# Two attention products in 64x32 tiles of the TensorE array, with units of every second head

## The chip, the cores and the metric

The kernel runs on one core of a Trainium2 chip. The metric is device microseconds from the start to the end of one execution. A core has five engines, each working through its own instructions in order: TensorE (PE, matmuls; its weight loads are shown as PEld), VectorE (DVE), ScalarE (ACT), GpSimd (POOL) and SyncE (SP, which issues the DMAs here). PE reads SBUF and writes PSUM, which has eight banks of 2 KB on each of 128 partitions. TensorE's clock is granted at one of two levels, 2.4 or 1.2 GHz; the profile writes them as 1.0 and 0.5.

## The reference

```python
batch, n_heads, seq, head_dim = (8, 8, 576, 64); n_mem = 32
def _attn_ref(q, k, v, phi):
    a = exp(phi - phi.max(axis=2)); a = a / (a.sum(axis=2) + 1e-09)     # over the 576 positions
    k_m, v_m = einsum('bhsm,bhsd->bhmd', a, k), einsum('bhsm,bhsd->bhmd', a, v)
    attn = softmax(q @ k_m.T / sqrt(64))                                 # over the 32 slots
    return attn @ v_m
def _moe_ref(x, w_in, w_out):  h = x @ w_in; return (h - tanh(h)) @ w_out     # 512 -> 2048 -> 512
def _moe2_ref(x, w_in, w_out): h = x @ w_in; return where(h > 0, h, exp(min(h, 0)) - 1) @ w_out
x = attn_out.transpose(0, 2, 1, 3).reshape(4608, 512); x = _moe_ref(x); x = _moe2_ref(x)
```

The weights come as 64-bit floats. Everything is computed to about fp32 accuracy.

## The kernel before

The program has an attention part, a first layer and a second layer. The attention runs beside the first half of the first layer, the second layer follows.

**Attention** works in 16 units: one batch `b` and four heads each (`Attention.unit`). A unit takes the maximum and the exponential of `phi`, forms `km` (k_m and v_m of its four heads, 32 array columns for each head), transposes q (`pq`) and k_m, v_m (`kT_ps`), forms the scores `sc`, and writes the probabilities `p`, each value as a high and a low part, to DRAM. The scores of two heads at a time are one product over all 128 rows of the array: `kT` holds the slots of a head twice, beside zeros, so that one pass serves two halves of q. A unit has two such products side by side (64 columns each) for each pair of heads, each into one bank.

**First layer.** v_m and w_in are multiplied first: `vw` = v_m times w_in, so that h = p times `vw`. w_in is cut in 8 column groups `pg` of 256, the work in 4 sweeps `sw` of two groups and 16 blocks `n` of 288 tokens, two blocks for each batch. The loop over `blocks` (index `bi`, 64 of them) does two steps `i` in each, one for each `pg`. A step is `h_unit` (12 matmuls, `h_ps`), the function h - tanh(h) on ACT, POOL and DVE (`g_a` to `g_d`), and up to two `x_unit`s of earlier blocks (12 matmuls each, `x_ps`, `x_next`). For the groups 0 to 3 `vw_whole` forms `vw` for one batch from plain fp32 operands, in two column halves of the array, with a v_m that holds zeros beside each head's block (`vbd`). For the groups 4 to 7 `vw_half` does it for two batches at once from high and low parts of v_m and w_in, three matmuls for each product. v_m is saved to DRAM and loaded again for the second half (`save_vm`, `load_vm`, `split_vm`).

**Conversion.** `convert` makes fp32 from the 64-bit weights, 128x512 words in a piece: one ACT and four DVE instructions through the one PSUM buffer of `cv_ps`; with `whole` the result stays fp32, otherwise ACT and POOL split it in high and low. Pieces are started by `Staged.round`, one in two rounds, from the queue `first` before the queue `todo`. `need(kind, pg)` runs rounds on the spot until the two pieces of a group are there. `raw_p` holds three pieces.

**What sets the order.** Each engine takes its instructions as the program issues them: `units.at` holds the round in which each unit begins, every `yield` of a unit ends one round, and `cv.round` advances the conversions. `misc`, three PSUM banks, serves `x_ps`, `vw_ps` and the attention's tiles alike; the product of `h_unit` has four banks of its own. `keep_busy` issues matmuls without a use, in places listed in `beside`.

Of the kernel before, what the change touches and what calls it, by code (L numbers as in the profile page):

```python
# [8 lines left out]
F32 = mybir.dt.float32  # L9
# [63 lines left out]
class Attention:  # L73
# [5 lines left out]
    def __init__(self, tc, ctx, const, ins, vm_dst, p_dram, side, psum):  # L79
        nc = tc.nc  # L80
        self.nc, self.ins, self.vm_dst, self.p_dram = nc, ins, vm_dst, p_dram
        self.ident, self.pmask, self.ones = const["ident"], const["pmask"], const["ones"]
# [16 lines left out]
        nc.gpsimd.memset(self.kT, 0.0)  # L99

    def load(self, u, what):
# [4 lines left out]
        view = lambda n, h0, n_h: self.ins[n][b, 4 * g + h0:4 * g + h0 + n_h].rearrange("h (p c) d -> p h c d", c=6)  # L106
# [12 lines left out]
    def unit(self, u, nxt, eng, first_p=None):  # L119
# [15 lines left out]
        beside = {("km", 2): 10, ("bmax", 3): 10, ("km", 3): 5, ("sc1", 2): 5, ("sc0", 3): 9, ("bmax", 5): 3}  # L135
# [42 lines left out]
        twice = lambda t: kmv[:, t].rearrange("p (o d) -> p o d", o=1).to_broadcast([128, 2, D])  # L178
# [9 lines left out]
        s = self.sc_p.tile([128, 18, M], F32, tag="s", name="s")  # L188
        for pr in range(2):
            qt = self.loaded.pop((u, f"q{pr}"))  # L190
            qT = wk.tile([128, 2, 3, 96], F32, tag="qT", name="qT")
            for h in range(2):
# [4 lines left out]
                nc.scalar.activation(qT[:, h], pq, ACTF.Copy)  # L197
# [3 lines left out]
            if pr == 0:  # L201
                kT_ps = ps_tile([128, 2, 128], "kT_ps")
                nc.tensor.transpose(kT_ps[:, 0, :], kk.rearrange("p h d -> p (h d)"), ident)
                nc.tensor.transpose(kT_ps[:, 1, :], vbd.rearrange("p h d -> p (h d)"), ident)
                for cp in range(2):
                    r = slice(64 * cp, 64 * cp + 64)
                    nc.scalar.activation(kT[r, :, cp, :], kT_ps[r, 0, :].rearrange("p (h m) -> p h m", h=4), ACTF.Copy)
                dst = self.vm_dst(b, g)
                src = kT_ps[:, 1, :].rearrange("p (r m) -> p r m", r=2)
                nc.scalar.activation(dst, src, ACTF.Copy)  # L210
                self.vm_done.add(u)
                yield
            sc_t = ps_tile([128, 512], "sc")
            sc = sc_t[:, :NB]
            for hq in range(2):
                if hq == pr:
                    keep_busy(nc, ident, sc_t[:, 384:], beside.get((f"sc{pr}", u), 0))
# [16 lines left out]
        pTv = r32(phl[:, :, 1])  # L234
        for r in range(2):
            nc.vector.transpose(pTv[:, r], s[:, 9 * r:9 * r + 9].rearrange("p j m -> p (j m)"))
        yield
        nc.scalar.activation(phl[:, :, 0], pTv, ACTF.Copy)
        eng.tensor_tensor(phl[:, :, 1], pTv, r32(phl[:, :, 0]), op=ALU.subtract)
# [3 lines left out]
        for c, t in enumerate(first_p or ()):  # L243
# [8 lines left out]
def make_const(nc, const):  # L252
# [3 lines left out]
    for h in range(4):  # L256
        for j in range(2):
            nc.vector.memset(pmask[32 * h:32 * h + 32, j:j + 1], 1.0 if h % 2 == j else 0.0)
# [696 lines left out]
```

## Time and profile before

| | |
|---|---|
| median of 3 runs | 1677.83 us (1676.79 to 1677.95) |
| span of the profiled execution | 1680.0 us |
| PE busy | 1616.5 us, 96% of the span |
| DVE, ACT, POOL busy | 1197.3, 930.9, 759.7 us |
| matmul records | 10038 |

The page gives the span of the profiled execution alone; what lies around it is in no view. A fp32 matmul stands in the trace as two records, a matmul of high and low parts as one. A line of a profile group reads: line of the source, engine, operation, output and inputs by name, shapes, count, then busy time (overlaps counted once) and the mean of one in ns, then the idle time of the engine before them and what ended it. A line of a timeline reads: start, time from the first start to the last end, engine, line, what it does, count, and in brackets the idle time before it with its releaser.

### The profile page before, as it was taken

The numbers are of one execution on the slowest core, as the hardware profiler recorded it, in microseconds if no ns is written. First come the engines' busy times: TensorE is split into PE (matmuls) and PEld (weight loads), VectorE is DVE, ScalarE is ACT, GpSimd is POOL, SyncE is SP. The second block draws the span as 40 slices with busy tenths as digits, with TensorE's granted clock in tenths as the row PEclk, the third lists the DMA queues.
The fourth block names the chain that finished last, engine by engine and source line by source line (L and its number), as shares of the span: only waits on it lengthen the run. The fifth ranks groups of instructions, "written<-read, shape, count | busy, mean of one in ns | idle before, by whom it ended". The sixth has DMA issues, their size and how long they took to land.

```text
span 1680.0 us, 26878 instructions
## 1 busy us (share of the span) xinstructions
PE 1616.5 (96%) x10038; PEld 1403.2 (84%) x10038; DVE 1197.3 (71%) x1746; ACT 930.9 (55%) x1677; POOL 759.7 (45%) x540
## 2 busy tenths in 40 slices
PE   6779999899999999999999999999999999999998
PEld 4558888787899999999999888888888888888886
DVE  6877688877989999999765655656565555555654
ACT  2546767777788898988853333333333333333332
POOL 1335656666767676767642322322232232323222
PEclk9889999999999999999999999999999999999999
DMA  9865667676565566665586321212121212121100
GB/s 237 211 188 169 208 194 232 194 230 208 192 199 174 171 220 217 218 220 193 174 319 253 101 76 38 88 38 75 47 67 51 63 51 64 50 76 51 32 7 25
DMA packets 140922, 236.10 MB, mean 141 GB/s; under 512 B 8184, under 2 KB 102392, under 8 KB 138744
## 3 DMA queue, kind: packets, MB, share of 16 engines
q1 hardware_dynamic: 140792, 234.39, 43.8%
q8 instruction: 79, 1.29, 0.3%
q14 instruction: 51, 0.42, 0.1%
HBM read 158.73 MB, written 74.45 MB: 139 GB/s over the span
## 4 chain that ended last, share of the span: by engine, by line
PE 70%; DVE 4%; issue 2%; ACT 2%; POOL 1%; DMA 0%; DVEq 0%; SPq 0%; POOLq 0%; ACTq 0%
PE h_ps L486 24%; PE o_ps L528 24%; PE x_ps L426 14%; PE h_ps L375 7%; PE vw_ps L344 1%; DVE s L403 1%; DVE vw L349 1%; DVE h_ps L402 1%; PE vw_ps L360 0%; DVE x L434 0%; DMA raw<-in_moe_w_in_dram 0%; DVE xr L460 0%; ACT t L386 0%; ACT vw L347 0%; ACT u L387 0%
## 5 line engine op out<-in xcount | busy, mean ns | idle before, releaser
L512 POOL TENSOR_TENSOR e<-hm,e 128x512 fp32r<-128x512 f32 x144 | 187.1, 1299 | 577.7 <-ACT e L511 534.5
L426 PE MATMUL x_ps<-g,w 128*128 128x288 f32 x3072 | 441.2, 297 | 7.4 <-ACT x L432 3.3
L426 PEld LDWEIGHTS x_ps<-g,w 128*128 128x128 f32 x3072 | 417.6, 189 | 20.2 <-ACT x L432 5.7
L486 PE MATMUL h_ps<-x,wi 128*128 128x512 f32 (+1 forms) x1920 | 424.6, 371 | 0.0
L528 PE MATMUL o_ps<-wo,e 128*128 128x512 f32 x1728 | 422.8, 393 | 0.7 <-POOL e L512 0.7
L486 PEld LDWEIGHTS h_ps<-x,wi 128*128 128x128 f32 x1920 | 336.1, 188 | 68.0
L528 PEld LDWEIGHTS o_ps<-wo,e 128*128 128x128 f32 x1728 | 323.4, 188 | 75.3 <-POOL e L512 1.1
L497 ACT ACTIVATE t_ps<-hm 128x512 f32<-128x512 f32 x144 | 86.7, 602 | 505.8 <-DVE hm L496 505.8
L393 POOL TENSOR_TENSOR v<-t,u 128x576 f32<-128x576 f32 x128 | 183.4, 1433 | 143.4 <-ACT u L387 134.3
L503 DVE SCALAR_TENSOR_TENSOR hm<-hm,t_ps 128x512 f32<-128x512 f32 x144 | 99.1, 688 | 200.3 <-ACT hm L498 200.3
L411 POOL TENSOR_TENSOR g<-s,g 128x576 fp32r<-128x576 f32 x128 | 200.6, 1567 | 81.1 <-ACT g L410 78.6
L375 PE MATMUL h_ps<-p,vw 128*128 128x288 f32 x1536 | 230.9, 299 | 1.3 <-DMA p<-phl 1.3
L375 PEld LDWEIGHTS h_ps<-p,vw 128*128 128x128 f32 x1536 | 210.8, 189 | 11.5 <-issue 8.1
L496 DVE TENSOR_SCALAR hm<-h_ps 128x512 f32<-128x512 f32 x144 | 99.6, 692 | 130.7 <-PE h_ps L486 129.7
L403 DVE SCALAR_TENSOR_TENSOR s<-s,v 128x576 f32<-128x576 f32 x128 | 146.5, 1144 | 6.3 <-POOL v L393 6.3
L386 ACT ACTIVATE t<-h_ps 128x576 f32<-128x576 f32 x128 | 83.4, 651 | 76.1 <-PE h_ps L375 31.7
L404 DVE COPY_PREDICATED s<-big,h_ps 128x576 f32<-128x576 uint32 x128 | 106.7, 834 | 11.8
L388 ACT ACTIVATE s<-u,bias 128x576 f32<-128x576 f32 x128 | 99.6, 778 | 26.0 <-POOL g L411 17.1
L505 DVE TENSOR_TENSOR hm<-hm,h_ps 128x512 f32<-128x512 f32 x144 | 98.9, 687 | 5.0
L504 DVE SCALAR_TENSOR_TENSOR hm<-hm,t_ps 128x512 f32<-128x512 f32 x144 | 98.9, 687 | 4.9
L498 ACT ACTIVATE hm<-hm 128x512 f32<-128x512 f32 x144 | 91.0, 632 | 13.1
L397 ACT ACTIVATE big<-u,bias 128x576 f32<-128x576 f32 x128 | 98.0, 765 | 0.1
(98 smaller groups left out, 1716.4 us busy)
## 6 DMA issues: line engine op xcount, KB each, us to landing
x_dram<-x SPq DMA_DIRECT2D x128, 288.0 KB
xr<-x_dram SPq DMA_DIRECT2D x72, 512.0 KB
p<-p_dram SPq DMA_DIRECT2D x62, 576.0 KB
raw<-in_moe_w_in_dram SPq DMA_DIRECT2D x32, 512.0 KB
raw<-in_moe_w_out_dram SPq DMA_DIRECT2D x32, 512.0 KB
w_dram<-wst SPq DMA_DIRECT2D x32, 512.0 KB
kv<-in_k_dram SPq DMA_DIRECT2D x16, 576.0 KB
kv<-in_v_dram SPq DMA_DIRECT2D x16, 576.0 KB
```

Of the source, the lines that this page charges most:

```text
L375: nc.tensor.matmul(ps[:, j, :NB], lhsT=vw[a][:, kc, 128 * j:128 * j + 128], rhs=p[:, kc, b, :], start=(k == 0), stop=(k == 5))
L388: nc.scalar.activation(s, u, ACTF.Square, bias=bias[:, 0:1], scale=G_S)
L393: nc.gpsimd.tensor_tensor(v, t, u, op=ALU.mult)
L403: nc.vector.scalar_tensor_tensor(s, s, G_B, v, op0=ALU.add, op1=ALU.mult)
L404: nc.vector.copy_predicated(s, big.bitcast(U32), d)
L411: nc.gpsimd.tensor_tensor(g[:, 1], s, r32(g[:, 0]), op=ALU.subtract)
L426: nc.tensor.matmul(ps, lhsT=wo[pg][a][:, j, 128 * dm:128 * dm + 128], rhs=self.g[n, pg][:, b, j, :], start=(k == 0), stop=(k == 11))
L486: nc.tensor.matmul(out, lhsT=w3[:, a, kc, 128 * j:128 * j + 128], rhs=x[:, b, kc, :], start=(i == 0), stop=(i == 11))
L496: nc.vector.tensor_scalar(hm, w[0], 0.0, None, op0=ALU.min)
L503: nc.vector.scalar_tensor_tensor(hm, hm, 1.0, t, op0=ALU.add, op1=ALU.mult)
L512: nc.gpsimd.tensor_tensor(e[:, 1], hm, r32(e[:, 0]), op=ALU.subtract)
L528: nc.tensor.matmul(acc, lhsT=e[:, a, jj, 128 * tg:128 * tg + 128], rhs=w4[:, b, j, :], start=(k == 0 and jj == 0 and i == 0), stop=(k == l ...
```

## The change

A unit now takes every second head of a batch (`view` reads `(h j)`, the unit's `g` picks `j`). k_m and v_m come out of the transpose in both halves of the partitions (`kvs`, formed by one instruction), so that the products can run in tiles of 64 rows and 32 columns: eight tiles hold four heads times two row halves, and no zeros are needed. The scores of all four heads are formed at once, after both pairs of q are transposed, into two banks. `vw_unit` replaces `vw_whole` and `vw_half`: one batch, one sweep (two groups `pg`), eight tiles in two banks, all from fp32. All eight groups of w_in stay whole fp32, v_m stays in SBUF, and its saving, loading and splitting are gone. `vw_unit` stands at each odd `bi`, for the next pair of blocks, between the step's two `x_unit`s. For the first two units the parts of `p` are written straight into the tiles that `h_unit` reads. The groups 4, 5 and 6, 7 of w_in are queued at block 26 and 30, not 24 and 28.

```diff
-        self.kT = fix.tile([128, 4, 2, M], F32, name="kT")
+        self.kT = fix.tile([128, 4, M], F32, name="kT")
...
-        kk = wk.tile([128, 2, D], F32, tag="kk", name="kk")
-        nc.vector.tensor_scalar(kk, twice(0), rs, None, op0=ALU.mult)
-        vbd = wk.tile([128, 2, D], F32, tag="vbd", name="vbd")
-        for j in range(2):
-            nc.vector.tensor_scalar(vbd[:, j], kmv[:, 1], rs, self.pmask[:, j:j + 1], op0=ALU.mult, op1=ALU.mult)
+        kvs = wk.tile([128, 2, 2, D], F32, tag="kvs", name="kvs")
+        twice = kmv[:, :2].rearrange("p t (o d) -> p t o d", o=1).to_broadcast([128, 2, 2, D])
+        nc.vector.tensor_scalar(kvs, twice, rs, None, op0=ALU.mult)
...
-            sc_t = ps_tile([128, 512], "sc")
-            sc = sc_t[:, :NB]
-            for hq in range(2):
-                nc.tensor.matmul(sc[64 * hq:64 * hq + 64], lhsT=kT[:, 2 * pr + hq].rearrange("p c m -> p (c m)"),
-                                 rhs=qT[:, hq].rearrange("p c q -> p (c q)"), start=True, stop=True)
-            nc.vector.transpose(s[:, 9 * pr:9 * pr + 9].rearrange("p j m -> p (j m)"), sc)
-            yield
+        sc = [ps_tile([128, 512], "sc") for _ in range(2)]
+        for h in range(4):
+            for cp in range(2):
+                r = slice(64 * cp, 64 * cp + 64)
+                nc.tensor.matmul(sc[cp][32 * h:32 * h + 32, :NB], lhsT=kT[r, h, :],
+                                 rhs=qT[r, h].rearrange("p c q -> p (c q)"), start=True, stop=True)
+        for cp in range(2):
+            nc.vector.transpose(s[:, 9 * cp:9 * cp + 9].rearrange("p j m -> p (j m)"), sc[cp][:, :NB])
+        yield
...
+    def vw_unit(self, vm, wi, b, pgs):
+        hi, lo = self.vw[b % 2, pgs[0] // 2]
+        ps = [self.misc.tile([128, 512], F32, tag="m", name="vw_ps") for _ in range(2)]
+        for pg in pgs:
+            cols = slice(256 * (pg % 2), 256 * (pg % 2) + 256)
+            for h in range(4):
+                for j in range(2):
+                    r = slice(64 * j, 64 * j + 64)
+                    nc.tensor.matmul(ps[j][32 * h:32 * h + 32, cols], lhsT=vm[r, b % 2, h, :], rhs=wi[pg][r, h, :],
+                                     start=True, stop=True)
+        cols = slice(256 * (pgs[0] % 2), 256 * (pgs[-1] % 2) + 256)
+        for j in range(2):
+            nc.scalar.activation(hi[:, j, cols], ps[j][:, cols], ACTF.Copy)
+            nc.vector.tensor_tensor(lo[:, j, cols], ps[j][:, cols], r32(hi[:, j, cols]), op=ALU.subtract)
...
-            staged, whole = [], (layer, kind) == (1, "i") and pg < 4
+            staged, whole = [], (layer, kind) == (1, "i")
...
-            if bi == 24:
+            if bi == 26:
                 cv.first.extendleft(reversed(conv_l1("i", 4, 5)))
-            if bi == 28:
+            if bi == 30:
                 cv.first.extendleft(reversed(conv_l1("i", 6, 7)))
...
+                if vw_next and (bi == 1 or i == 0):
+                    vb, vsw = vw_next
+                    pgs = [2 * vsw + i] if bi == 1 else [2 * vsw, 2 * vsw + 1]
+                    for vpg in pgs:
+                        need("i", vpg, bi == 1)
...
+                    make_vw(vb, pgs)
```

Three places show how it moves instructions.

On SP, the DMAs around the first two units' stores: `in_moe_w_out` rows are the pieces of w_out, two for each group, `in_moe_w_in` those of w_in. Before:

```order
L603 DMA raw<-in_moe_w_out_dram 128x512
L246 DMA p<-phl 32x1152 x4
L247 DMA p_dram<-phl 128x1152
L246 DMA p<-phl 32x1152 x4
L247 DMA p_dram<-phl 128x1152
L116 DMA q<-in_q_dram 96x2x384
L603 DMA raw<-in_moe_w_out_dram 128x512
L113 DMA phi<-in_phi_dram 96x4x192
L600 DMA raw<-in_moe_w_in_dram 128x2x256
```

The two rows of w_out are the third and the fourth of it, with which the groups 0 and 1 are complete, ahead of w_in's groups 2 and 3. After:

```order
L575 DMA raw<-in_moe_w_out_dram 128x512
L242 DMA p_dram<-p 128x576 x2
L572 DMA raw<-in_moe_w_in_dram 128x2x256
L116 DMA q<-in_q_dram 96x2x384
L113 DMA phi<-in_phi_dram 96x4x192
L321 DMA p<-p_dram 128x1152
```

The third piece of w_out stands where it stood, but w_in's group 2 comes next. A unit has one `yield` less, so the opening has one round less, and the fourth piece (group 1) stays in `todo`, behind all that block 0 puts in `first`.

On DVE, around the `vw` of group 2 in block 1 (L50 to L57 are one conversion, the L57 row ends it). Before:

```order
L54 SCALAR_TENSOR_TENSOR cv_m<-raw,cv_m 128x512
L57 SCALAR_TENSOR_TENSOR w_838<-raw,cv_m 128x512
L236 STREAM_TRANSPOSE phl<-s 128x288 x2
L145 TENSOR_REDUCE nmax<-mT 128x1
L363 TENSOR_TENSOR vw<-vw_ps,vw 128x512
L402 TENSOR_TENSOR h_ps<-h_ps,t 128x2x288
```

After:

```order
L342 TENSOR_TENSOR vw<-vw_ps,vw 128x256 x2
L50 TENSOR_SCALAR cv_m<-cv_m 128x512
L51 TENSOR_SCALAR cv_m<-cv_m 128x512
L54 SCALAR_TENSOR_TENSOR cv_m<-raw,cv_m 128x512
L57 SCALAR_TENSOR_TENSOR w_862<-raw,cv_m 128x512
```

The four conversion rows stand seven times in a row there before the next `h_ps` row: both pieces of w_in's group 3, four pieces of w_out's groups 2 and 3, and last the fourth piece of w_out, which the first `x_unit` needs. On PE that `x_unit` stands right behind this `vw`, as before.

On DVE, in block 31, the first with a `vw` of group 4 and 5. Before, ahead of the first `vw` of that sweep:

```order
L434 COPY x<-x_ps 128x288
L402 TENSOR_TENSOR h_ps<-h_ps,t 128x2x288
L403 SCALAR_TENSOR_TENSOR s<-s,v 128x576
L404 COPY_PREDICATED s<-big,h_ps 128x576
L349 TENSOR_TENSOR vw<-vw_ps,vw 64x512 x2
```

After:

```order
L384 COPY_PREDICATED s<-big,h_ps 128x576
L54 SCALAR_TENSOR_TENSOR cv_m<-raw,cv_m 128x512
L57 SCALAR_TENSOR_TENSOR w_6312<-raw,cv_m 128x512
L342 TENSOR_TENSOR vw<-vw_ps,vw 128x512 x2
L414 COPY x<-x_ps 128x288
```

The last piece of group 5 (`w_6312`) now ends right before the evictions of the product that reads it. On PE the product stands behind the first of the step's two `x_unit`s. Block 35 has the same for group 7.

## Rows read from the trace of the kernel before

**Rows 1.** Stretches: limits, length, busy of the five engines, PEclk, DMA share, GB/s.

```profile
97.61:152.66 55.05, 45.05 (x388) 37.18 (x386) 44.73 (x75) 35.34 (x71) 30.64 (x22) 0.96 0.58 176
152.66:430.00 277.34, 259.71 (x2194) 225.77 (x2191) 219.33 (x342) 206.41 (x415) 176.69 (x126) 1.00 0.68 212
430.00:512.00 82.00, 81.17 (x604) 75.33 (x603) 74.41 (x105) 65.97 (x115) 56.66 (x40) 1.00 0.59 192
512.00:830.00 318.00, 316.83 (x2386) 314.73 (x2385) 295.48 (x418) 281.34 (x488) 222.74 (x155) 1.00 0.57 199
830.00:1680.00 850.00, 843.13 (x3962) 699.78 (x3961) 494.18 (x677) 305.60 (x516) 251.72 (x177) 1.00 0.24 80
```

**Rows 2.** Groups by line: `vw` matmuls of fp32 parts, a conversion's low part, evictions of `vw`.

```profile
L64 POOL TENSOR_TENSOR w<-cv_a,w 128x512 fp32r<-128x512 f32 x24 | 31.5, 1312 | 0.0
...
L344 PE MATMUL vw_ps<-w,vms 128*128 128x256 f32 x192 | 28.7, 285 | 1.2 <-DVE vw L349 1.0
...
L363 DVE TENSOR_TENSOR vw<-vw_ps,vw 128x512 fp32r<-128x512 f32 x32 | 21.7, 682 | 30.1 <-ACT vw L362 30.1
...
L362 ACT ACTIVATE vw<-vw_ps 128x512 fp32r<-128x512 f32 x32 | 18.8, 592 | 14.5 <-PE vw_ps L360 14.5
```

**Rows 3.** Timeline of PE, 303 to 323 us.

```profile
303.37 0.71 PE L218 MATMUL sc<-qT,kT 128*64 128x288 f32 x4
304.01 1.86 PE L426 MATMUL x_ps<-g,w 128*128 128x288 f32 x12
...
313.70 1.75 PE L426 MATMUL x_ps<-g,w 128*128 128x288 f32 x12
315.38 1.08 PE L360 MATMUL vw_ps<-w,vm 128*64 128x256 f32 x8
316.40 1.86 PE L426 MATMUL x_ps<-g,w 128*128 128x288 f32 x12
319.32 2.16 PE L170 MATMUL km<-kv,a 96*32 96x192 f32 x48 [1.06 <-ACT a L163]
321.41 1.08 PE L360 MATMUL vw_ps<-w,vm 128*64 128x256 f32 x8
```

**Rows 4.** Timeline of PE, 601 to 624 us.

```profile
601.73 0.88 PE L344 MATMUL vw_ps<-w,vms 128*128 128x256 f32 x6
602.44 1.78 PE L375 MATMUL h_ps<-p,vw 128*128 128x288 f32 x12
...
620.43 3.36 PE L426 MATMUL x_ps<-g,w 128*128 128x288 f32 x24
623.63 1.77 PE L375 MATMUL h_ps<-p,vw 128*128 128x288 f32 x12
```

**Rows 5.** Timeline of DVE, the same stretch.

```profile
619.57 0.69 DVE L57 SCALAR_TENSOR_TENSOR cv_a<-raw,cv_m 128x512 uint32<-128x512 uint32 x1
...
622.06 0.83 DVE L404 COPY_PREDICATED s<-big,h_ps 128x576 f32<-128x576 uint32 x1
```

**Rows 6.** Timeline of PE: the first `h_unit`, the first `x_unit`, the ninth block step.

```profile
59.95 1.86 PE L375 MATMUL h_ps<-p,vw 128*128 128x288 f32 x12 [1.35 <-DMA p<-phl]
...
94.56 3.25 PE L426 MATMUL x_ps<-g,w 128*128 128x288 f32 x12
97.61 0.68 PE L195 MATMUL pq<-ident,q 96*128 96x96 f32 x3
...
152.66 1.85 PE L375 MATMUL h_ps<-p,vw 128*128 128x288 f32 x12
```

**Rows 7.** Timeline of ACT: the first instruction of three conversions.

```profile
28.34 0.64 ACT L48 ACTIVATE cv_m<-raw 128x512 f32<-128x512 f32 x1 [0.92 <-DVE w L57]
...
31.93 0.63 ACT L48 ACTIVATE cv_m<-raw 128x512 f32<-128x512 f32 x1 [1.87 <-DVE w L57]
...
38.40 0.63 ACT L48 ACTIVATE cv_m<-raw 128x512 f32<-128x512 f32 x1 [5.36 <-DMA raw<-in_moe_w_in_dram]
```

**Rows 8.** Timeline of DVE: the end of w_in's group 2.

```profile
87.98 0.69 DVE L57 SCALAR_TENSOR_TENSOR w<-raw,cv_m 128x512 uint32<-128x512 uint32 x1
```

More of the change, by code (lines that the diff above doesn't have):

```diff
@@ L254, in make_const @@
     make_identity(nc, ident)
-    pmask = const.tile([128, 2], F32, name="pmask")
-    for h in range(4):
-        for j in range(2):
-            nc.vector.memset(pmask[32 * h:32 * h + 32, j:j + 1], 1.0 if h % 2 == j else 0.0)
     ones = const.tile([128, 96], F32, name="ones")
@@ L329, in load_p, with new_vw @@
         self.nc.sync.dma_start(out=r32(t).rearrange("p r t s -> p (r t s)"),
-                               in_=self.p_dram[n // 2, :, :, n % 2].rearrange("g q m f -> (g q) m f"))
-    def vw_half(self, vm, wi, pg, po):
+                               in_=self.p_dram[n // 2, n % 2].rearrange("p g f -> p (g f)"))
+    def new_vw(self, b, sw, slot):
+        self.vw[b % 2, sw] = [self.vw_p.tile([128, 2, 512], F32R, tag=f"vw{slot}{t}", name="vw") for t in range(2)]
+    def vw_unit(self, vm, wi, b, pgs):
@@ L333, in vw_half @@
         nc = self.nc
-        pars = range(2)
-        if po == 0:
-            for par in pars:
-                pool = self.vw2_p if self.vw2_p and par and pg // 2 % 2 else self.vw_p
-                self.vw[par, pg] = [pool.tile([128, 2, 256], F32R, tag=f"vw{pg % 2}_{par}{t}", name="vw")
-                                    for t in range(2)]
-        ps = self.misc.tile([128, 2, 256], F32, tag="m", name="vw_ps")
-        for kc in range(2):
-            p = 2 * po + kc
-            for i, (a, b) in enumerate(((0, 0), (0, 1), (1, 0))):
-                nc.tensor.matmul(ps[:, kc], lhsT=vm[:, a, p, :], rhs=wi[b][:, p, :], start=(i == 0), stop=(i == 2))
@@ L370, in h_unit @@
             keep_busy(nc, self.const["ident"], ps[:, 1, 384:], 9)
+        c0 = 256 * (pg % 2)
         for j in range(2):
@@ L563, in moe_kernel @@
         new = lambda stack, name, n, **kw: stack.enter_context(tc.tile_pool(name=name, bufs=n, reuse_waits="tile", **kw))
-        l1a, l1b, l1c, at0_ctx, at1_ctx, wt_ctx, late_ctx, pro, ps_h_ctx = (ExitStack() for _ in range(9))
+        l1a, l1b, l1c, at0_ctx, at1_ctx, wt_ctx, pro, ps_h_ctx = (ExitStack() for _ in range(8))
         m1 = Moe1(tc, l1a, const, p_dram, x2_dram)
         wt_p = {0: new(l1b, "wt0", 1, side="right"), "early": new(l1a, "wte", 1)}
-        vm_p = new(l1b, "vm", 2, side="right")
-        vms_p = new(l1b, "vms", 1, side="right")
+        vm_p = new(l1b, "vm", 1, side="right")
         cv_p = new(l1b, "cv", 2, side="right")
@@ L613, in dst @@
                         if kind == "i":
-                            ws[pg] = [wt_p[pg2 % 2].tile([128, 4, 256], F32 if whole else F32R, tag=f"wi{odd}a", name="w1")]
-                            if not whole:
-                                ws[pg].append(wt_p[2].tile([128, 4, 256], F32R, tag=f"wl{pg}", name="w1"))
+                            ws[pg] = [wt_p[pg2 % 2].tile([128, 4, 256], F32, tag=f"wi{odd}a", name="w1")]
                         else:
@@ L693, in moe_kernel @@
         blocks += [(ss, bp, sub, j) for ss, bp, sub in groups[4:] for j in range(4)]
-        vw_first = {4 * b + 2 * sub - 1: (b, sub) for b in range(4) for sub in range(2)}
         LAG = 4
@@ L806, in moe_kernel @@
                 nxt = (2 * nss + nsub, 4 * nbp + nj)
[L808 to L816 removed]
+            vw_next = None
+            if bi % 2 and nxt:
+                vw_next = (nxt[1] // 2, nxt[0])
             if at0_open:
@@ L866, in moe_kernel @@
                     m1.g_d(*pend.pop())
[L867 to L870 removed]
+                if vw_next and (bi == 1 or i == 0):
[3 more added lines that the diff above has]
+                        need("i", vpg, bi == 1)
                     while not all(u in vm_done for u in range(2 * vb + 2)):
                         units.round()
[L873 to L879 removed]
+                    if i == 0:
+                        m1.new_vw(vb, vsw, bi // 2 % 2 ^ 1)
+                    make_vw(vb, pgs)
                 if soon and bi > 60:
```

149 lines of the change are left out of this document (37 added, 112 removed).

## The prediction

> **What bounds the kernel now.** I read the stretches first [rows 1], to see which engine is full where. PE is busy 259.71 of 277.34 us from 152.66 to 430, 81.17 of 82 up to 512, 316.83 of 318 up to 830 and 843.13 of 850 in the second layer, which the change does not touch. So from 152.66 on, PE time that goes is time that goes, unless a new wait takes its place. DVE is next: 295.48 of 318 in the saturated stretch. Ahead of 152.66 it is different: from 97.61 on PE is busy for 45.05 of 55.05 us, the rest are waits for conversions and for the attention. There PE work is worth little and the order of the other engines much. Then I read the timelines of PE for the price of one product [rows 3, 4], those of the opening [rows 6 to 8] for what the new order does, and DVE's timeline and groups [rows 2, 5] for the evictions. The result is worked out as a difference and taken off the median, 1677.8; the profiled span, 1680.0, is 0.1% longer.
>
> **The price of a product in array tiles.** A `vw` of the old kind has 8 records in two column halves, four behind one another in each, 256 columns wide, and the next instruction starts 316.40 - 315.38 = 1.02 us after it [rows 3]. A scores product has two records behind one another, 288 columns wide, and takes 304.01 - 303.37 = 0.64 us. From 1024 k + o = 1.02 and 576 k + o = 0.64 come k = 0.85 ns for a column of one record and o = 0.15 us. `km` tests this: 48 records in four column tiles, 12 in each of 192 columns, give 2304 x 0.85 + 150 = 2.11 us, and 321.41 - 319.32 = 2.09 was measured. So column tiles work side by side at no cost, and it is the records of one tile that count. Around such a product PE loses some more: 0.08 us ahead of it (the `x_unit` before it holds PE 315.38 - 313.70 = 1.68 us; two of them undisturbed take 3.20, so 1.60) and 0.11 us behind it (1.86 for the next `x_unit`, against 1.75) [rows 3, 4]. A `vw` product costs 1.21 us in all, a scores product 0.83.
>
> **What goes on PE**, if the two row halves work side by side as the column tiles do. Before, groups 0 to 3 have 32 products of 1.21 = 38.7 us. After, 14 pairs of groups have four records in each tile, 1.21 each; the two single groups of the opening stand side by side, 1.21; the two of block 1 stand apart, 512 x 0.85 + 150 = 0.59 and 0.19 for the edges, 1.56. Sum 19.7, less by 19.0. Groups 4 to 7 have 32 products of 602.44 - 601.73 = 0.71 us [rows 4], 22.7 in all, with no edges since they use the whole array; after, 16 pairs of 1.21 are 19.4, less by 3.3. Scores: 32 of 0.83 before, 16 after, less by 13.3. Together 35.6 us of PE. Row halves side by side are in no row of this trace. Below, the cost may be what it would be one after the other, which is the second rival; I take the value next to the column tiles. The Trainium skill ("TensorE: Matmul & The Clock Gate", Part 3, Packing small matmuls) says that tiles in different rows and columns run concurrently; no run here shows it for rows, and by that page the sum is the one I use.
>
> **Up to the ninth step (152.66 before).** Behind this mark lie 26 of the old `vw` of groups 0 to 3, 13 pairs now, and 21 of the old scores products, 11 now: 13 x 1.21 + 10 x 0.83 = 24.0 us less. The other 19.0 + 13.3 - 24.0 = 8.3 lie ahead of it, and I expect them to be swallowed. The order rows show why: the fourth piece of w_out now waits in `todo`, and the first `x_unit` calls for it in block 1, so six other pieces are converted first, seven in a row, with PE standing. One conversion takes 31.93 - 28.34 = 3.59 us from first instruction to first instruction, with the one PSUM buffer [rows 7]. Before, w_in's group 2 was done at 87.98 + 0.69 = 88.7 [rows 8]. The opening gets some 2.5 us shorter: the first `h_unit` waited 1.35 us for the DMA of `p` [rows 6], which now needs none, and one conversion's half less stands ahead (bounds 0 and 4). From 86.2, seven conversions reach 111.3; the high part on ACT, about as long as the 0.64 of a conversion's first instruction, and the low part on POOL, 1.31 [rows 2], put it at 113.3. The `x_unit` ended at 97.6 before [rows 6]. From there to the ninth step PE had 45.05 us of work in 55.05; now 1.6 less for `vw`, 1.7 less for scores, 1.0 less since it ran partly at the lower clock level (0.96 in the row), 1.9 more for matmuls of `keep_busy` that stood earlier before: 42.6 us. Six of the conversions that DVE had here are done, so I fill PE as in the next stretch, 259.71 / 277.34 = 0.94: 45.5 us. The ninth step comes at 159, 6 us later. Bounds: with the idle share of before (55.05 less 45.05 = 10 us) it comes 13 us later; with PE full and the opening 4 us shorter, at the old time. Also one unit's `km` (2.1 us) has moved behind this mark.
>
> **From there to 830.** PE gets 24.0 + 3.3 - 2.1 = 25.2 us shorter. What is late instead:
> First, banks. `misc` has three. A `vw` or scores product now holds two. In the two steps in which `km` still holds the third, the `x_unit` right behind `vw` gets a bank that this `vw` has just filled, and waits for ACT's copy and DVE's subtraction, 592 and 682 ns [rows 2], and for what DVE has ahead of it: 2.2 us each, 4.4. Some five times the next small product takes a bank whose scores DVE has yet to transpose, 0.6 each, 3. Together 7.5 (bounds 2, if DVE is free each time, and 14, if its queue is as long as in the saturated stretch).
> Second, blocks 31 and 35. The last piece of group 5, then of group 7, ends on DVE right ahead of its use. In the nearest step of before, the copy on DVE that stands ahead of it ends at 622.89 and two conversion instructions of 0.70 follow, 624.3 [rows 5]; PE would be at the product after the first `x_unit`, 620.43 + 1.60 = 622.0 [rows 4]. Wait 2.3 each, 4.6 (bounds 2 and 7).
> Third, in the rest of the saturated stretch PE waited 1.0 us for DVE's `vw` [rows 2]; that goes, since 64 evictions of 64 rows become 32 of 128. The second `x_unit` of a step now needs the bank of the first, whose copy ends about when `vw` does: 0.2 each time, 16 times. Net 1.5 (bounds -1 and 6).
> ACT and POOL lose eight splits and the four of v_m, and SP the seven DMAs of v_m; they are not on the path and count nothing.
>
> **Sum.** 6 - 25.2 + 7.5 + 4.6 + 1.5 = -5.6 us, so 1677.8 - 5.6 = 1672.
>
> **Rivals.**
> (a) Everything is gained: seven conversions cost nothing net, because PE idled there anyway, and DVE is early at each bank. 0 - 25.2 + 2 + 2 - 1 = -22: 1656, and down to 1642 if the 8.3 and the opening come back too. For it: PE is 99% full where most of the gain lies. Chance 0.14.
> (b) The other side: the row halves take turns. Then every tile pair has twice the records: 30 x 1024 x 0.85 ns = 26 for the pairs, 2 for the singles, 16 x 576 x 0.85 = 8 for the scores, 36 us more: 1708. It turns slower once the halves overlap by less than about five sixths. For it: no row shows row tiles. Against it: records of different column tiles start next to each other at no cost. Chance 0.11.
> (c) The burst is longer. A conversion waited 5.36 us for its piece [rows 7]; if DMA makes each of the seven 4.5 us, not 3.6, that is 6 us more, and PE, idle so long, comes back at the lower level, 2 to 4 more: 1681. Chance 0.15.
> (d) The evictions become the bound: every pair waits for its copies, 592 + 682 ns, 30 times 1.27 = 38, of which 4.4 and 3.2 are in the sum: 1702. For it: DVE is at 93% in the saturated stretch. Against it: it loses 32 x 0.68 us there, and only at two places does the next tile need that bank. The Trainium skill ("TensorEngine Tiling (Array Packing)", PSUM Bottleneck) warns of exactly this: array tiles speed up TensorE and not the emptying of PSUM. The trace has one sign for it, the 1.0 us on DVE's `vw` above. Chance 0.05.
>
> **How the numbers follow.** The forecast has 0.55. Its own bounds, 13, 14, 7 and 6 at one end and 0, 2, 2 and -1 at the other, do not meet all at once; 1660 to 1686 holds most of it. The range goes to (a) and past (c) and leaves out (b), (d) and the end of (a): 1651 to 1692. A difference of 0.2%, 3.4 us, is about what a measurement can tell. Of the forecast I count 0.40 as faster, 0.08 same and 0.07 slower, of (c) 0.03, 0.05 and 0.07, (a) is faster, (b) and (d) slower: faster 0.57, same 0.13, slower 0.30.
>
> **What would show it.** `vw` at 1.02 us for 16 records of each pair on PE (twice that in case b); scores at 0.64 once for each unit; a gap of 20 us or more on PE ahead of the first `x_unit`, released by a conversion's low part, and seven conversions 3.6 us apart under it; the ninth `h_unit` near 159; 2 us waits for DVE in blocks 31 and 35; the second layer unchanged. A ninth step at 152 or earlier, or PE idle of over 25 us between it and 430, would prove the sum wrong.

## The result and the profile after

The changed kernel takes 1696.1 us (1695.1 to 1697.9), the kernel before 1677.9 in the same series: ratio 1.0104, 95% interval 1.009 to 1.0118. It is slower by 18 us, where 1672 was forecast, and the time lies above the range. Steps are counted by the starts of the first layer's `h_unit`s, from 0; the ninth is step 8, step 127 is the last. The stretches of both traces between the same steps (limits, length, busy of PE, PEld, DVE, ACT and POOL, PEclk, DMA share, GB/s), after first:

```profile
60.00:160.11 100.11, 63.10 (x608) 53.17 (x607) 69.94 (x109) 49.65 (x97) 40.70 (x29) 0.80 0.50 147
160.11:521.58 361.47, 331.19 (x3122) 296.08 (x3121) 277.97 (x428) 267.75 (x522) 230.38 (x164) 0.98 0.66 207
521.58:600.79 79.21, 77.51 (x670) 73.64 (x669) 69.13 (x97) 61.83 (x109) 46.56 (x33) 1.00 0.51 173
600.79:622.82 22.03, 17.61 (x110) 17.16 (x109) 14.83 (x22) 12.66 (x23) 9.75 (x8) 0.85 0.33 103
622.82:874.58 251.76, 249.25 (x2151) 240.24 (x2150) 202.80 (x296) 200.37 (x355) 174.44 (x118) 1.00 0.61 207
874.58:1694.00 819.42, 812.39 (x3770) 674.29 (x3768) 472.24 (x653) 287.22 (x485) 236.07 (x167) 1.00 0.23 75
```

```profile
60.00:152.66 92.66, 73.35 (x610) 58.35 (x610) 73.08 (x122) 52.92 (x105) 44.35 (x32) 0.91 0.67 186
152.66:508.31 355.65, 337.19 (x2767) 297.41 (x2764) 290.19 (x440) 269.34 (x524) 230.07 (x163) 1.00 0.66 207
508.31:586.65 78.34, 78.11 (x590) 77.50 (x589) 73.98 (x108) 69.40 (x121) 54.48 (x39) 1.00 0.54 175
586.65:602.44 15.79, 15.79 (x122) 15.79 (x121) 15.28 (x22) 14.57 (x27) 14.07 (x10) 1.00 0.59 217
602.44:855.59 253.15, 252.21 (x1899) 250.72 (x1897) 231.65 (x320) 219.15 (x380) 173.02 (x120) 1.00 0.60 211
855.59:1680.00 824.41, 817.54 (x3770) 674.19 (x3768) 472.30 (x653) 286.87 (x485) 236.16 (x167) 1.00 0.23 74
```

Step 8 comes 7.45 us later; from there to step 60, where most was to be gained, the changed kernel needs 5.8 us more: PE is busy 6.0 us less and idle 11.8 us more (30.3 against 18.5). Steps 75 to 78 lose 6.2; the rest of the first layer gains 0.5, the part from step 127 on 5.0. That sums to the 14.1 by which the profiled spans differ (the profiled execution of before is the longest of its four, 1681.4).

**The price** is as forecast. PE's timeline in the saturated stretch (start, length, idle before it and releaser):

```profile
626.11 1.09 PE L337 MATMUL vw_ps<-w,vm 64*32 64x256 f32 x32
627.14 1.87 PE L406 MATMUL x_ps<-g,w 128*128 128x288 f32 x12
```

The next instruction starts 1.03 us after the pair, and the pair does the work of two old products of 1.02 [rows 3]. Undisturbed scores take 0.65 us for a whole unit, what one of its two products took before. In noburst, a run described below, it reads:

```profile
100.06 0.72 PE L212 MATMUL sc<-qT,kT 64*32 64x288 f32 x16
100.70 1.86 PE L355 MATMUL h_ps<-p,vw 128*128 128x288 f32 x12
```

The row halves work side by side.

**The burst** is as forecast too. PE around the first `x_unit`, and ACT's first instruction of two of the conversions:

```profile
84.14 2.53 PE L406 MATMUL x_ps<-g,w 128*128 128x288 f32 x9
110.88 0.61 PE L406 MATMUL x_ps<-g,w 128*128 128x288 f32 x1 [24.21 <-ACT w L62]
112.68 0.85 PE L406 MATMUL x_ps<-g,w 128*128 128x288 f32 x2 [1.19 <-POOL w L64]
```

```profile
84.81 0.66 ACT L48 ACTIVATE cv_m<-raw 128x512 f32<-128x512 f32 x1
88.42 0.62 ACT L48 ACTIVATE cv_m<-raw 128x512 f32<-128x512 f32 x1 [2.95 <-DVE w L57]
```

The conversions are 3.61 us apart (3.59 in [rows 7]). The instruction behind the `x_unit` starts at 113.3 (forecast 113.3; 97.6 before, [rows 6]), and step 8 at 160.1 (forecast 159).

**What was not forecast** is inside the pairs. PE and ACT around one of them:

```profile
239.70 0.38 PE L200 MATMUL kT_ps<-ident,kvs 128*128 128x128 f32 x2
240.76 0.62 PE L337 MATMUL vw_ps<-w,vm 64*32 64x256 f32 x2 [0.69 <-ACT x L412]
241.75 1.09 PE L337 MATMUL vw_ps<-w,vm 64*32 64x256 f32 x30 [0.37 <-ACT vm L203]
242.77 1.86 PE L406 MATMUL x_ps<-g,w 128*128 128x288 f32 x12
```

```profile
239.64 0.78 ACT L368 ACTIVATE s<-u,bias 128x576 f32<-128x576 f32 x1
240.32 0.39 ACT L412 ACTIVATE x<-x_ps 128x288 f32<-128x288 f32 x1
240.61 0.76 ACT L377 ACTIVATE big<-u,bias 128x576 f32<-128x576 f32 x1
241.28 0.26 ACT L201 ACTIVATE kT<-kT_ps 128x128 f32<-128x128 f32 x1
241.44 0.26 ACT L203 ACTIVATE vm<-kT_ps 64x128 f32<-64x128 f32 x1
```

The pair's first matmul waits for the bank of the `x_unit` ahead, which ACT copies (`x`, L412) behind its work for the function h - tanh(h), called the gate below. Its second writes the other bank, that of `kT_ps`, free only when ACT has copied `vm` at 241.70. It waits for the bank and not for this `vm`: the pair is that of batch 2, the copy that of batch 4. So 30 of 32 records start 0.99 us behind the first, and the pair holds PE 2.01 us, with 0.69 of idle time ahead of it. Of the 0.99 the profile shows 0.37 as idle; the rest looks busy, because the first two records run alone. From step 8 to 60 the second matmul is late like this in 7 of the 13 pairs and in 6 of the 11 units' scores, released by a copy on ACT each time. Summed over PE's timeline from step 8 to 60, the 13 pairs take 21.8 us from their start to the point where PE is done or waits for the next instruction, with 2.4 idle ahead and 7.4 behind: 31.7. The 26 products of before took 26.6, 3.1 and 2.6: 32.4. Scores: 11 units take 19.6 with what is idle around them, 21 products took 15.4. Of the 24.0 us that the sum counts here, none is left.

Behind such waits the granted clock falls as well, which [rows 1] had at 1.00:

```profile
207.04 0.62 PE L337 MATMUL vw_ps<-w,vm 64*32 64x256 f32 x2 [0.36 <-ACT x L412]
208.57 1.09 PE L337 MATMUL vw_ps<-w,vm 64*32 64x256 f32 x30 [0.92 <-ACT qT L193]
211.12 3.25 PE L406 MATMUL x_ps<-g,w 128*128 128x288 f32 x12 [1.45 <-DVE vw L342]
214.17 0.68 PE L191 MATMUL pq<-ident,q 96*128 96x96 f32 x3
214.55 2.92 PE L355 MATMUL h_ps<-p,vw 128*128 128x288 f32 x12
```

During the third of these waits, at 210.1, the clock goes to its lower level, and it stays there for 6.8 us: an `x_unit` holds PE for 3.05 us (half of the 3.20 for two in [rows 4] is 1.60). It falls for 6.8 us again at 347, where `km` has waited 3.40 us for ACT, and at 610, behind **a late conversion**:

```profile
602.37 2.92 PE L406 MATMUL x_ps<-g,w 128*128 128x288 f32 x21
606.83 0.40 PE L406 MATMUL x_ps<-g,w 128*128 128x288 f32 x1 [1.54 <-ACT w L62]
610.11 0.85 PE L406 MATMUL x_ps<-g,w 128*128 128x288 f32 x2 [2.88 <-POOL w L64]
610.76 3.08 PE L355 MATMUL h_ps<-p,vw 128*128 128x288 f32 x12
613.64 4.54 PE L406 MATMUL x_ps<-g,w 128*128 128x288 f32 x24
```

It is the second piece of w_out's group 7, which the last of these `x_unit`s in step 75 needs. By the program's order it is converted in step 75; before, in step 72.

### The profile page after: what moved, and what is told of

Its sections match the earlier page's. It is cut to its first block, busy times and chain, and to the rows that moved or that the text cites. A ratio compares the mean times of both kernels' runs of the same rounds, so it can differ in the third digit from the quotient of the medians.

```text
span 1694.1 us, 28080 instructions
## 1 busy us (share of the span) xinstructions
PE 1589.7 (94%) x10742; PEld 1382.9 (82%) x10742; DVE 1146.7 (68%) x1680; ACT 896.6 (53%) x1623; POOL 745.2 (44%) x526
## 4 chain that ended last, share of the span: by engine, by line
PE 60%; POOL 5%; DVE 4%; ACT 3%; issue 3%; DMA 1%; POOLq 0%; ACTq 0%; DVEq 0%
PE h_ps L466 24%; PE o_ps L508 23%; PE x_ps L406 9%; PE h_ps L355 4%; POOL g L391 2%; POOL v L373 2%; DVE s L383 1%; POOL wst L64 1%; DVE s L384 1%; DVE h_ps L382 1%; DMA x_dram<-x 1%; ACT t L366 1%; ACT x L412 1%; ACT big L377 1%; ACT g L390 0%
## 5 line engine op out<-in xcount | busy, mean ns | idle before, releaser
L406 PE MATMUL x_ps<-g,w 128*128 128x288 f32 x3072 | 448.6, 298 | 45.8 <-ACT w L62 25.8
L355 PEld LDWEIGHTS h_ps<-p,vw 128*128 128x128 f32 x1536 | 214.8, 192 | 2.9 <-issue 2.4
L383 DVE SCALAR_TENSOR_TENSOR s<-s,v 128x576 f32<-128x576 f32 x128 | 137.5, 1074 | 12.5 <-POOL v L373 12.5
L382 DVE TENSOR_TENSOR h_ps<-h_ps,t 128x576 f32<-128x576 f32 x128 | 96.7, 755 | 13.4 <-ACT u L367 13.4
```

What stands on the lines that cost most here:

```text
L355: nc.tensor.matmul(ps[:, j, :NB], lhsT=vw[a][:, kc, c0 + 128 * j:c0 + 128 * j + 128], rhs=p[:, kc, b, :], start=(k == 0), stop=(k == 5))
L382: nc.vector.tensor_tensor(d, d, t, op=ALU.subtract)
L383: nc.vector.scalar_tensor_tensor(s, s, G_B, v, op0=ALU.add, op1=ALU.mult)
L406: nc.tensor.matmul(ps, lhsT=wo[pg][a][:, j, 128 * dm:128 * dm + 128], rhs=self.g[n, pg][:, b, j, :], start=(k == 0), stop=(k == 11))
```

## The experiments

**The burst: noburst, before_burst, burst_units4, o7only.** noburst puts the fourth w_out piece ahead again:

```diff
-                cv.first.extend(conv_l1("i", 2, 3) + conv_l1("o", 2, 3))
+                cv.first.extend(list(cv.todo) + conv_l1("i", 2, 3) + conv_l1("o", 2, 3))
+                cv.todo.clear()
```

> The changed kernel, with the fourth piece of w_out's first two groups put ahead of w_in's groups 2 and 3 again, so that the first x_unit of block 1 calls for no other conversion. Theory A (the seven conversions in a row cost what the traces show between the third and the ninth step, 7 us, and all behind them is bound by PE): the gap of 24 us ahead of the first x_unit is gone, the ninth h_unit starts at 152 to 155 us, not 160, and the time is 1689. Theory B (the other units only come later, and the work that waited is caught up behind the ninth step, where PE stands 30 us up to step 60): the ninth step is earlier but the time stays within 2 us of 1696.

1674.9 us, ratio to before 0.9967 (0.9956 to 0.9979): 21 us less than the changed kernel, and 0.3% under the kernel before. Step 8 comes at 153.8. Both theories miss the size: 6.3 us come back by step 8, 3.3 more by step 60, 7.6 at steps 75 to 78, where the late piece is not late any more, and 2.3 from there to step 127, where in the changed kernel eight `x_unit`s wait 2.4 us for ACT's copies. Then the reverse, before_burst:

```diff
-        cv = Staged([conv(1, "i", 1, 1)] + conv_l1("o", 0, 1), 2)
+        cv = Staged([conv(1, "i", 1, 1)] + conv_l1("o", 0) + [conv(1, "o", 1, 0)], 2)
...
-                cv.first.extend(conv_l1("i", 2, 3) + conv_l1("o", 2, 3))
+                cv.first.extend(conv_l1("i", 2, 3) + conv_l1("o", 2, 3) + [conv(1, "o", 1, 1)])
```

> The kernel before, with the fourth w_out piece of its first two groups put behind w_in's groups 2 and 3 and w_out's 2 and 3, as the changed kernel has it: the first x_unit of block 1 then calls for a run of conversions. The pieces of w_out's group 7 stay as early as they were. Theory A (noburst gained 21 us, of which 6 to 7 lie ahead of the ninth step, 3 behind it up to step 60, and the rest comes from w_out's last group, which got late only because the attention units were stepped less often during the burst): 6 to 10 us more than before, 1686 to 1689. Theory B (the burst alone is worth the 21): 1698.

1717.0, ratio 1.023 (1.0208 to 1.0251): 39 us more than before, and more than either theory has. Step 8 comes 14.3 us later, step 60 already 36. A part of it is a block whose `p` comes late (PE's timeline, step 52); the rest was not taken apart:

```profile
499.56 3.22 PE L375 MATMUL h_ps<-p,vw 128*128 128x288 f32 x12 [6.38 <-DMA p<-p_dram]
```

What a burst leaves behind is an attention that is late. `need` at block 1's `vw` calls the units' rounds along with the conversions, `need` in an `x_unit` doesn't. In noburst and in the kernel before the units have had 32 rounds by step 4, in the changed kernel 28 and in before_burst 29, and in these two the last attention output is stored in step 50, not 48 (the expectation of yield_sc below writes 52 and 50 for it). Until then the attention's pool holds the memory of w_out's group 7. burst_units4 keeps the burst and gives the units their four rounds:

```diff
                 for i in range(2):
                     need("o", 2 * sw + i)
+                for _ in range(4 if (sw, n, dm) == (0, 0, 0) else 0):
+                    units.round()
```

> The changed kernel with its run of seven conversions kept, but four rounds of the attention units called behind it, so that the units stand where noburst has them (in the changed kernel's order the last attention output is stored two steps later than in noburst, because the conversions of w_in's groups 2 and 3 called the units along and those called by an x_unit do not). Theory A (of noburst's 21 us, PE's standing in the run itself is worth the 6.3 by which the ninth step comes earlier; the rest, 3.3 up to step 60 and 11 behind it, comes from the four rounds that the units lost, the late pieces of w_out's group 7 among it): 1679 to 1683. Theory B (the standing itself and its aftermath cost the 21): 1693 to 1697.

1688.5, ratio 1.0066 (1.0049 to 1.0084): between the theories. Its step 60 (521.7) is that of the changed kernel, so the four rounds gain nothing up to there, and noburst's gain up to there is PE's standing in the burst. At step 78 it is 7.6 us ahead: that is the four rounds. o7only speeds up the late piece alone:

```diff
-                if bi < 7:
+                if bi < 7 or bi in (27, 28):
                     cv.round()
```

> The changed kernel with nothing but two more rounds of conversions in each of blocks 27 and 28 (four in all), so that the last pieces of w_out's group 7 are ready before step 66, not step 76. Theory A (the late piece costs its waits of 1.5 and 2.9 us and about 2 to 3 at the lower clock behind them): 1689 to 1691. Theory B (the rounds take DVE and ACT where they are full): 1694 to 1697.

1687.0, ratio 1.0054 (1.0039 to 1.0069): 9.1 us less, somewhat more than theory A has, and no wait for a conversion at steps 75 to 78. It undoes the same loss as the four rounds. o7early puts the same rounds of conversions into noburst, where that loss is gone already:

> As noburst, and four more rounds of conversions in blocks 27 and 28, so that the last two pieces of w_out (group 7) are converted some ten steps before the second layer's half of w_out asks for them. Theory A (the late piece costs its own two waits, 1.5 and 2.9 us, and half of the 6.8 us at the lower clock level behind them): no wait for a conversion at steps 75 to 78, no drop of the clock there, 6 us less than noburst: 1683. Theory B (the extra rounds take DVE and ACT where they are full, and PE waits there instead): no more than 2 us less than noburst.

1677.2, ratio 0.9982 (0.9966 to 0.9998), 2 us more than noburst and so theory B: the rounds are worth nothing by themselves. By the medians some 8 of noburst's 21 us are this late piece and 13 the standing; the traces give each about half: 9.6 us up to step 60, which the four rounds don't bring, and 7.6 and 2.3 behind it, which both they and o7only bring (the 2.4 us of waits for ACT's copies are in neither).

**The root: yield_sc.** One line in the changed kernel:

```diff
...
+        yield
         s = self.sc_p.tile([128, 18, M], F32, tag="s", name="s")
```

> The changed kernel with one line more: a yield ahead of the scores, so that a unit has as many rounds as it had in the kernel before (the two scores products of before had a yield between them). Nothing is moved by hand: by the order of the program the opening has its round back, the fourth w_out piece is converted ahead of w_in's groups 2 and 3, and the last attention output is stored at step 50, not 52. Theory A (the missing round is the root of the burst and of the late w_out, and it also puts the scores only one round behind the last pq, whose copy on ACT frees the second bank): as noburst, and the 4.5 us inside its scores groups go, 1667 to 1671. Theory B (those waits only move on to the next tile, as vwfirst's did): 1673 to 1677, as noburst.

1676.5, ratio 0.9981 (0.9961 to 1.0): as noburst, theory B. The root of burst and late w_out is the yield that went with the second scores product. The other half of theory A falls: the scores groups go on waiting (13.2 us for 11 units, 11.7 for 10 in noburst).

**The banks: shared4, before_shared4, bank4, sbuf3.** shared4 is noburst with one pool of four banks, from which the conversion's scratch comes too:

```diff
-        misc = m1.misc = new(top, "ps_m", 3, space=PSUM)
-        cv_ps = new(top, "ps_c", 1, space=PSUM)
+        misc = m1.misc = new(top, "ps_m", 4, space=PSUM)
+        cv_ps = misc
...
```

> noburst (1674.9), with the conversion's PSUM scratch tile taken from the same pool as x_ps, vw_ps, sc and the others: four banks shared, where three and one were kept apart. The scratch stays in PSUM, so ACT and DVE work as in noburst. Theory A (waits for the second bank of a pair, and for the bank right behind it, are what the array tiles lose: in noburst's stretch from the ninth step to step 60 some 5.8 us inside the vw groups, 4.5 inside the scores groups and up to 14 behind them): a conversion holds a bank for part of the time only, so half to most of it goes, 8 to 15 us: 1660 to 1667. Theory B (ACT and DVE are late with what they copy, and PE meets the lateness one tile further on, whatever the number of banks): 1672 to 1678.

1662.6, ratio 0.9909 (0.989 to 0.9928): theory A, 12 us under noburst (10 by the ratios). The stretch from step 8 to 60, noburst and shared4 (columns as above):

```profile
153.78:511.92 358.14, 328.21 (x3051) 295.40 (x3048) 275.70 (x421) 263.85 (x512) 226.53 (x161) 0.98 0.65 203
```

```profile
151.57:498.58 347.01, 321.73 (x3052) 290.92 (x3049) 279.35 (x421) 263.43 (x511) 225.99 (x161) 0.99 0.68 209
```

11.1 us of the gain lie here. The pairs hold PE 16.1 us (19.1 in noburst), idle behind them falls from 7.2 to 1.6, ahead of `x_ps` from 11.5 to 3.8. `km`'s waits grow from 8.8 to 11.3. The edit also lets a conversion have more than one bank; what this and the fourth bank are worth without pairs, the same edit in the kernel before shows:

> The kernel before, with the same four shared banks as shared4: the conversion's scratch taken from the pool of x_ps and the others. Theory A (the bank waits belong to the products that take two banks at once; the old vw and scores take one each, and wait 5.7 and 2.0 us in all between the ninth step and step 60): within 3 us of the kernel before, 1675 to 1679. Theory B (a fourth bank helps any order of this work, so that shared4's 12 us say nothing of pairs): 1664 to 1669.

1675.4, ratio 0.9983 (0.9971 to 0.9995): 3 to 4 us less than before, theory A. Its stretch from step 8 to 60:

```profile
149.25:504.21 354.96, 336.98 (x2768) 298.75 (x2764) 294.11 (x440) 269.54 (x524) 228.36 (x163) 1.00 0.68 207
```

That is 0.7 us less than the 355.65 of before; the gain lies ahead of step 8, which comes 3.4 us earlier. So a fourth bank is worth some 7 us more where pairs are used, and between step 8 and 60, where the pairs wait, 11.1 against 0.7. bank4 and sbuf3 try the same on the changed kernel with the conversion's scratch in SBUF:

```diff
...
-        cv_ps = new(top, "ps_c", 1, space=PSUM)
+        cv_ps = new(l1b, "cv_m", 1, side="right")
...
```

> The changed kernel with a fourth PSUM bank in the pool of x_ps, vw_ps, sc, km and the others; the conversion's scratch tile stands in SBUF instead of PSUM. Burst and late w_out stay as they are. Theory A (a pair of banks out of three is what costs: between the ninth step and step 60 the trace has 8.2 us inside the vw groups and 5.4 inside the scores groups, ahead of the second bank, some 8 more right behind the groups, and two drops of the clock of 3.4 us each): the groups come to 1.02 to 1.10 (vw) and 0.72 (scores), the waits behind them go, the stretch between the ninth step and step 60 is some 20 us shorter than 361.5, and the time is 1676. Theory B (ACT and DVE are late with what they have to copy, whatever the bank, so that PE meets the same lateness one tile further on): within 4 us of 1696, with the waits put down to x_ps, pq or km instead. Theory C (the row halves cost PE something by themselves): the groups stay at 1.4 and more.

> The control of bank4: the conversion's scratch tile stands in SBUF, but the pool keeps three banks (one bank of PSUM is unused in the first layer). Every theory: if the place of the scratch tile costs nothing, 1696 within 2; if ACT and DVE handle it at another speed, the difference to 1696 is what has to be taken off bank4's.

1733.9 and 1748.2: a fourth bank gives 14 us between the two, but the scratch in SBUF costs 52 (below), so that bank4 alone tells nothing.

**The order: vwfirst, serial.** vwfirst places the pair ahead of the first `x_unit`:

```diff
...
+                ahead = 1 < bi < 27 and vw_next and i == 0 and all(u in vm_done for u in range(2 * vw_next[0] + 2))
+                if ahead:
+                    vw_now(i)
                 x_next(True)
...
```

> noburst, with the vw pair of blocks 3 to 25 placed right behind the h_unit, ahead of the step's first x_unit and of the attention's small tile, instead of behind both: its two banks are then the ones let go longest ago, not the ones that the x_unit or a small tile has just filled. Theory A (banks): the vw groups of that stretch come to 1.02 to 1.10 from a mean of 1.47, some 5 us less inside them, and a part of the waits of 1.45 right behind them goes as well: 1666 to 1670. Theory B (lateness of ACT and DVE moves on to the next tile): 1673 to 1677.

1680.7, ratio 1.0016 (1.0004 to 1.0028): 6 to 8 us more than noburst, which neither theory had. The pairs are as theory A has them, 13.5 us for 13; the `x_unit` behind pays:

```profile
230.81 1.09 PE L337 MATMUL vw_ps<-w,vm 64*32 64x256 f32 x32
234.56 3.83 PE L406 MATMUL x_ps<-g,w 128*128 128x288 f32 x17 [2.66 <-DVE vw L342]
```

Idle ahead of `x_ps` from step 8 to 60 grows from 11.5 to 18.0. So here the wait was moved, not removed. serial was to take the overlap of the row halves away:

```diff
...
-        for pg in pgs:
...
-            for h in range(4):
-                for j in range(2):
...
+        for j in range(2):
...
+            for pg in pgs:
...
+                for h in range(4):
...
```

> noburst, with the matmuls of the vw pairs and of the scores put in another order: all of the first row half and its bank, then all of the second, so that the row halves no longer overlap; same matmuls, same banks. On PE this costs 30 x 1.02 us for the pairs, about 1 for the two single groups of block 1 and 16 x 0.6 for the scores, 41 us, if PE sets the time everywhere; the wait for the second bank then lies beside the first half's work. Theory A (banks): between the ninth step and step 60 up to 10 of its 19 us come back, because the waits inside the groups vanish: 1700 to 1708. Theory B (the waits are no matter of banks): all of it shows, 1712 to 1716. If row halves never overlapped in the first place, nothing changes: 1675.

1679.7, ratio 1.0006 (0.9993 to 1.002): 5 to 7 us more than noburst, for a reason that was not looked into. It didn't do what it was made for: PE overlapped the halves nevertheless (below), so it says nothing of the two theories.

**What is left: yield_sc4**, yield_sc with shared4's banks.

> yield_sc with the four shared banks of shared4. Theory A (banks and the round of the scores are two separate losses): 4 us below shared4, 1656 to 1660. Theory B (with four banks the scores find a bank anyway, or the waits that are left are those for data, for ACT's exp ahead of km above all, which a yield ahead of the scores doesn't touch): 1661 to 1665.

1662.5, ratio 0.9885 (0.9847 to 0.9924): the median is that of shared4, the ratio 4 us better, and the interval holds both theories. The profiled execution, the shortest of four (1657.1 to 1665.7), speaks for theory A from step 8 to 60:

```profile
150.11:492.73 342.62, 319.88 (x3068) 290.05 (x3065) 278.78 (x422) 263.71 (x512) 230.18 (x162) 0.99 0.69 214
```

That is 4.4 us less than in shared4, with the scores at 8.9 us for 11 units (12.6 for 10 in shared4). Whether these 4 us are there on the median stays open. Of the 24.0 us of PE work that the sum takes off between step 8 and 60, shared4 shows 8.6 (355.65 to 347.01) and this execution 13.0. The longest wait left there in shared4 is one of `km`:

```profile
271.59 4.07 PE L170 MATMUL km<-kv,a 96*32 96x192 f32 x48 [3.81 <-ACT g L390]
```

`km` needs the exponential, which ACT takes behind the gate's work; this reading was not put to a test. shared4 and yield_sc4 are the fastest versions found, 15 to 19 us under the kernel before.

**The second layer: pad32, before_pad32.** The 5.0 us behind step 127 were to be unchanged work. pad32 (on noburst) and before_pad32 add a constant that nothing reads and that takes 32 bytes of each partition:

```diff
+    pad = const.tile([128, 2], F32, name="pad")
+    nc.gpsimd.memset(pad, 0.0)
     ones = const.tile([128, 96], F32, name="ones")
```

> noburst with a constant of 32 bytes per partition more, that nothing reads: all tiles of the left side, the four left w34 tiles and x of the second layer among them, then begin at the same addresses, modulo 64 bytes, as in the kernel before (they moved by 32 bytes when pmask went). From step 127 on the same matmuls take 824.4 us in the kernel before and its variants and 819.4 to 819.7 in every variant of the changed kernel. Theory A (it is the addresses): 824 from step 127 on, and the time about 5 us over noburst's 1674.9: 1680. Theory B (it is something else, such as the state in which the first layer leaves the queues): 819 to 820 and 1675.

> The kernel before with the same constant of 32 bytes more, which puts its left tiles where the changed kernel's stand, modulo 64 bytes. Theory A: 819 to 820 us from step 127 on, 1673 in all, and 1 to 2 us less if the first layer's matmuls gain by it too. Theory B: 824 and 1678.

From step 127 on, noburst and pad32:

```profile
854.99:1674.70 819.71, 812.39 (x3770) 674.33 (x3768) 472.53 (x653) 287.20 (x485) 236.15 (x167) 1.00 0.23 75
```

```profile
854.92:1679.90 824.98, 817.54 (x3770) 674.27 (x3768) 472.95 (x653) 287.40 (x486) 236.68 (x167) 1.00 0.23 75
```

pad32 takes 1679.6 (1.0, 0.9988 to 1.0013), theory A: the 5 us are addresses. before_pad32 gains 2.7 of them behind step 127 (821.75) and takes 1677.1 (0.9981, 0.9965 to 0.9998), half of theory A: its addresses agree with the changed kernel's modulo 64 bytes, not modulo 128.

## Why the prediction was wrong, step by step

- **Price on PE** (1.02 for a pair, 0.64 for scores): right. Rival (b), row halves in turns, is out.
- **Up to the ninth step** (+6): right, 7.45. But the sum let the burst end there. That it took rounds from the units was seen only as "one unit's `km`" of 2.1 us; that w_out's group 7 waits for the attention's end was not followed through the order. Some 8 to 10 us, and 3.3 more of standing up to step 60.
- **Banks** (7.5, bounds 2 and 14): this step failed most. From step 8 to 60 the sum has -24.0 + 2.1 + 7.5 = -14.4; +5.8 was measured, 20 us apart, of which the burst explains 3.3. At undisturbed prices the pairs and scores there are 13 x 1.02 + 11 x 0.65 = 20.4 us, and with their waits they take 31.7 + 19.6 = 51.3: 30.9 us of waits in them and around them. The products of before had 32.4 + 15.4 less 26 x 1.02 + 21 x 0.64, 7.8 us. So the term that was put at 7.5 came to 23. The step asked only who waits behind a pair, and for DVE. The larger part of the 23 is the wait inside the pair or the scores for the second bank (8.5 us in 13 pairs, 6.1 in 11 units), filled by the `x_unit` or the small tile right ahead and emptied by ACT behind the gate's instructions. A product of one bank has no second bank to wait for: the 26 of before took 26.6 us, 1.02 each. A fourth bank brings back 11 of the 20 us, and 0.7 in the same stretch of the kernel before. What the remaining 6 are made of stays open.
- **Clock**: a term that was missing. Before, it was full from step 8 on; now it drops at 210, 347 and 610, 6.8 us each time. At half the clock that is an estimate of at most 3.4 us of PE work for each drop.
- **Blocks 31 and 35** (4.6): 1.6, two waits of 0.8 for DVE. Steps 60 to 75 and 78 to 127 together give 0.5 us where the sum has a loss of 2.8. (By its own terms the third item there is 16 x 0.2 - 1.0 = 2.2, not 1.5, and the early bound of the ninth step comes out 2 us late, not at the old time; neither decides.)
- **Second layer unchanged**: wrong by 5.0 in the forecast's favour, through addresses.
- **Rivals**: (a) is out. (c) is out too, with conversions 3.61 us apart, though PE did come back at a lower clock (0.80 from 60 us to step 8, 0.91 before). (d) had the mechanism by half, with the evictions of the pair in place of the copies ahead of it, at 0.05. The Trainium skill ("TensorEngine Tiling (Array Packing)", PSUM Bottleneck) warns that with array tiles the emptying of PSUM may become the bottleneck; the trace agrees for the stretch beside the attention (21.8 us for 13 pairs), and not for the saturated one, where a pair stands at 1.03.
- **The test named** did speak: it asked for over 25 us of idle time between the ninth step and 430 us, and PE idles 26.8 us there (17.6 before).

## What to carry to other kernels

A product that takes two banks at once out of a pool of three waited here for whatever stood right ahead of it: before counting PE's saving, write down for each new tile which earlier tile held its bank, who empties it and what that engine does first. A yield that goes from a generator shifts every table that counts rounds; follow the last user of each resource that it frees, not only the place where the order first differs. And compare the unchanged part of the program by itself, since 32 bytes of a constant were worth 5 us there.

## What the runs showed of the hardware

**Row halves overlap in both orders that were run.** In serial all matmuls of one half stand ahead of the other's in the program, and the pair takes as long:

```profile
510.06 1.12 PE L337 MATMUL vw_ps<-w,vm 64*32 64x256 f32 x32
511.11 1.86 PE L406 MATMUL x_ps<-g,w 128*128 128x288 f32 x12
```

1.05 us to the next instruction, against 1.03. The first half has two matmuls on each column tile; if PE started matmuls in the program's order, the second half could begin only behind the start of the later ones, but its first records start 0.05 us after the pair's first.

**DVE on SBUF alone stands still beside POOL.** The conversion's last instruction, scratch in PSUM (after) and in SBUF (sbuf3), 160 to 850 us (count, busy, mean ns, idle):

```profile
L57 DVE SCALAR_TENSOR_TENSOR cv_a<-raw,cv_m 128x512 uint32<-128x512 uint32 x40 | 27.5, 688 | 1.4
```

```profile
L57 DVE SCALAR_TENSOR_TENSOR cv_a<-raw,cv_m 128x512 uint32<-128x512 uint32 x39 | 65.6, 1682 | 1.4
```

Of sbuf3's 64 instructions of this line 36 took over 0.9 us, 1.92 on the mean, and POOL was busy in 98% of that time; in that of the other 28, in 20%. With the scratch in PSUM POOL was busy in 65% of this line's time, and none of the 64 took over 0.7 us. The Trainium skill ("SBUF — State Buffer", SBUF: two separate sides) says that a DVE instruction with two SBUF inputs and a GpSimd one that reads SBUF lock each other out; the trace agrees. L51, which reads the scratch alone, grew too, from 699 to 1079 ns; why is not shown.

**Addresses count for PE.** The same 3770 matmul records take 812.4 or 817.5 us by where their tiles begin (noburst and pad32). Which operand it is was not tried.
